# Seven block products for eight in one pair of output chunks of batches 2 to 7, with both packed casts of a slot on ScalarE

## The chip, the cores and the metric

The kernel runs on one core of a Trainium2 chip. The metric is the device time of one execution in microseconds. TensorE multiplies matrices into PSUM, VectorE (DVE) and ScalarE (ACT) do elementwise work and read PSUM, GpSimd (POOL) does elementwise work in SBUF and issues the input transfers, SyncE (SP) issues the output transfers and the transposing transfers.

## The reference

Attention through 32 packed vectors per head, then a layer with h * cos(h) as its activation. There are 8 batches, 8 heads, 576 tokens, a head width of 64; the layer is 512 -> 2048 -> 512 over 4608 tokens.

```python
p_packed = sm_attn(p, k, v)                  # 32 packed vectors per head
out = sm_attn(q, p_packed, p_packed)         # back to 576 tokens
x = transpose(out, (0, 2, 1, 3)).reshape(B * S, H * D)
h = x @ w_in                                 # 512 -> 2048
g = h * cos(h)
return g @ w_out                             # 2048 -> 512
```

## The kernel before

The packed vectors are multiplied by w_in first (PPW), so that h comes straight from the second attention's weights a2n and PPW. All matmuls take bf16 and sum in fp32. The kernel goes through the batches in steps. Step s computes attention and g of batch s, while TensorE is kept fed from a "filler": the output matmuls of batch s-1. A step has a front (scores, sums, normalisation, with pieces of filler) and a slot (16 h products, each followed by a quota of filler). PSUM has three double-bank tiles "psA" and two single banks "ot".

```python
A = ctx.enter_context(tc.tile_pool(name="psA", bufs=3, space=PSUM))
O = ctx.enter_context(tc.tile_pool(name="psO", bufs=2, space=PSUM))
...
def normalise(b):
    a2n[b] = a2n_pool.tile([128, 2, S], BF16, name="a2n", tag="a2n")
    for y in range(2):
        ACT.activation(out=lns[b][:, y], in_=lns[b][:, y], func=AF.Exp, scale=-1.0)
    for y in range(2):
        V.scalar_tensor_tensor(out=a2n[b][:, y], in0=a2u[b][:, y], scalar=r1[b][:, y:y + 1],
                               in1=lns[b][:, y], op0=ALU.mult, op1=ALU.mult)
...
def h_mm(b, fc):
    ps = psa()
    for y in range(2):
        for e in range(2):
            nc.tensor.matmul(ps[:, e, 0:HS], PPW[b][:, y, fc * 128:(fc + 1) * 128],
                             a2n[b][:, y, e * HS:(e + 1) * HS], start=(y == 0), stop=(y == 1))
    ...
    ACT.activation(out=csv, in_=ps[:, :, 0:HS], func=AF.Sin, bias=PI_HALF)
    def rest():
        V.tensor_tensor(out=gT[b][:, fc, :]..., in0=ps[:, :, 0:HS], in1=csv, op=ALU.mult)
        if fc % 8 == 7:          # the last 64 tokens go to a tile shared by two batches
            G.tensor_copy(out=joint[b // 2][...], in_=gT[b][:, fc - 7:fc + 1, 512:576])
    return rest
...
def out_gen(b):                  # the filler: chunks of 128 tokens, 512 columns at a time
    groups = [(0, 1), (2,), (3,)] if b == 0 else [(c,) for c in range(n_chunks(b))]
    for grp in groups:
        pss = {c: O.tile([128, DM], FP32, name="ot", tag="ot") for c in grp}
        ...
            nc.tensor.matmul(pss[c], w, w_out_bf[:, fc, :], start=(fc == 0), stop=(fc == NFC - 1))
            if fc == NFC - 1:
                copy(out_eng[...], osb, pss[c]); nc.sync.dma_start(out=rows, in_=osb[a:z, :])
            yield                # one unit of filler
```

Chunk 4 (the joint tile of two batches) is computed whole with the odd batch, so that a batch has 4 or 5 chunks of 16 units. A step from 3 on is:

```python
fill(1000); set_filler(s - 1)
permute_v(s + 1)                              # GpSimd
s2(s); ppw(s, 2, V); xbar("q", s + 1)
fill(10)
s1(s + 1); ppw(s, 3, V); a1_xbar(s + 1); recips(s + 1); ...
fill(4);  sums2(s, 0)
fill(5);  sums2(s, 1)
normalise(s)
ACT.preload_act_table_set(SIN_SET)
fill(13)
load(...)                                     # v, q of s + 2, k of s + 3
slot(s, [(5, lambda: pp(s + 1, engs=(ACT, ACT))), (10, lambda: pw2(s + 1))], 5, {10: 3})
```

In the slot, pp (the packed vectors of the next batch) comes after h 5 and pw2 (two packed products with their casts to bf16, one by VectorE and one by ScalarE) after h 10. The last line leaves five units for the end of the slot and gives h 10 a fourfold share.

Of the kernel before, what the change touches and what calls it, by code (L numbers as in the profile page):

```python
# [8 lines left out]
FP32 = mybir.dt.float32  # L9
# [6 lines left out]
def kernel(  # L16
# [10 lines left out]
    nc = tc.nc  # L27
    B, H, S, D = q.shape
# [5 lines left out]
    TP = S // C  # L34
    HS = S // 2
    PSUM = bass.MemoryType.PSUM
    EXP_SET = "natural_log_exp_and_others"
    SIN_SET = "trig_and_small"

    const = ctx.enter_context(tc.tile_pool(name="const", bufs=1))  # L40
    bf_pool = ctx.enter_context(tc.tile_pool(name="bf", bufs=1))
    vp_pool = ctx.enter_context(tc.tile_pool(name="vp", bufs=2))
    att_pool = ctx.enter_context(tc.tile_pool(name="att", bufs=1))
    a2n_pool = ctx.enter_context(tc.tile_pool(name="a2n", bufs=2))
    ppw_pool = ctx.enter_context(tc.tile_pool(name="ppw", bufs=2))
    g_pool = ctx.enter_context(tc.tile_pool(name="g", bufs=2))
    j_pool = ctx.enter_context(tc.tile_pool(name="joint", bufs=2))
    cos_pool = ctx.enter_context(tc.tile_pool(name="cos", bufs=3))
    o_pool = ctx.enter_context(tc.tile_pool(name="o", bufs=4))
# [8 lines left out]
    w_out_bf = const.tile([128, NFC, DM], BF16, name="w_out_bf")  # L58
    ident = const.tile([128, 128], BF16, name="ident")
# [3 lines left out]
    p_raw = const.tile([128, 2 * B, D], FP32, name="p_raw")  # L63
# [84 lines left out]
    def recips(b):  # L148
        r1[b] = small.tile([128, 2], FP32, name="r1")
        rs1[b] = small.tile([128, 2], FP32, name="rs1")  # L150
        V.reciprocal(r1[b], sums1[b])
        V.tensor_scalar(out=rs1[b], in0=r1[b], scalar1=scale, scalar2=None, op0=ALU.mult)
# [42 lines left out]
    def ppw(b, n, eng=None, own=False, later=False, cuts=((0, 512),)):  # L195
        if b not in PPW:
            PPW[b] = ppw_pool.tile([128, 2, DF], BF16, name="PPW", tag="PPW")
        two = isinstance(eng, tuple)
        if own:
            ps = [bank(), bank()]  # L200
        else:
            t = psa()
            ps = [t[:, 0, :], t[:, 1, :]]
        for x in range(4):
            for y in range(2):
                r = slice(64 * y, 64 * y + 64)
                nc.tensor.matmul(ps[y][32 * x:32 * x + 32, :], ppT[b % 2][r, 2 * x + y, :],  # L207
                                 w_in_bf[r, x, n * 512:(n + 1) * 512], start=True, stop=True)

        def evacuate(cuts=cuts):  # L210
            if own or two:
                for a, z in cuts:
                    for y in range(2):
                        copy(eng[y] if two else eng, PPW[b][:, y, n * 512 + a:n * 512 + z], ps[y][:, a:z])
            else:
                copy(eng or (V, ACT)[n % 2], PPW[b][:, :, n * 512:(n + 1) * 512], t)
        if later:
            return [lambda c=c: evacuate((c,)) for c in cuts]
        evacuate()

    def s2(b):
        a2u[b] = att_pool.tile([128, 2, S], BF16, name="a2u", tag="a2u")
        ps = scores(ppT[b % 2], xT["q", b])
        for y in range(2):
            ACT.activation(out=a2u[b][:, y].rearrange("p (e x) -> p e x", e=2),  # L225
                           in_=ps[y][:, :, 0:HS], func=AF.Exp, scale=rs1[b][:, y:y + 1])

    def sums2(b, y):
        if b not in lns:
            lns[b] = att_pool.tile([128, 2, S], FP32, name="lns", tag="lns")  # L230
        ps = psa()
        for e in range(2):
            nc.tensor.matmul(ps[:, e, 0:HS], ones_blk, a2u[b][:, y, e * HS:(e + 1) * HS],  # L233
                             start=True, stop=True)
        ACT.activation(out=lns[b][:, y].rearrange("p (e x) -> p e x", e=2),  # L235
                       in_=ps[:, :, 0:HS], func=AF.Ln)

    def normalise(b):
        a2n[b] = a2n_pool.tile([128, 2, S], BF16, name="a2n", tag="a2n")
        for y in range(2):  # L240
            ACT.activation(out=lns[b][:, y], in_=lns[b][:, y], func=AF.Exp, scale=-1.0)  # L241
        for y in range(2):
            V.scalar_tensor_tensor(out=a2n[b][:, y], in0=a2u[b][:, y], scalar=r1[b][:, y:y + 1],  # L243
                                   in1=lns[b][:, y], op0=ALU.mult, op1=ALU.mult)
# [3 lines left out]
    def h_mm(b, fc):  # L248
        if fc == 0:
            gT[b] = g_pool.tile([128, NFC, S], BF16, name="gT", tag="gT")  # L250
            if b % 2 == 0:
                joint[b // 2] = j_pool.tile([128, NFC, 128], BF16, name="joint", tag="joint")
        ps = psa()
        for y in range(2):
            for e in range(2):
                nc.tensor.matmul(ps[:, e, 0:HS], PPW[b][:, y, fc * 128:(fc + 1) * 128],  # L256
                                 a2n[b][:, y, e * HS:(e + 1) * HS], start=(y == 0), stop=(y == 1))
        cs = cos_pool.tile([128, S], BF16, name="cosT")
        csv = cs.rearrange("p (e x) -> p e x", e=2)
        ACT.activation(out=csv, in_=ps[:, :, 0:HS], func=AF.Sin, bias=PI_HALF)  # L260

        def rest():
            V.tensor_tensor(out=gT[b][:, fc, :].rearrange("p (e x) -> p e x", e=2),  # L263
                            in0=ps[:, :, 0:HS], in1=csv, op=ALU.mult)
            if fc % 8 == 7:
                j0 = (b % 2) * 64
                G.tensor_copy(out=joint[b // 2][:, fc - 7:fc + 1, j0:j0 + 64],  # L267
                              in_=gT[b][:, fc - 7:fc + 1, 512:576])
        return rest

    n_out, out_eng = [0], [V, ACT]

    def pieces_of(b, c):
        ob = out[b * S:(b + 1) * S, :].rearrange("(p c) d -> c p d", c=C)
        if c == 4:
            o0 = out[(b - 1) * S:b * S, :].rearrange("(p c) d -> c p d", c=C)
            return [(0, 64, o0[5, 32:96]), (64, 128, ob[5, 32:96])]
# [8 lines left out]
    def n_chunks(b):  # L286
        return 5 if b % 2 and b < B - 1 else 4

    def tail_chunk(b, c):
        osb = o_pool.tile([128, DM], FP32, name="osb")  # L290
        for i in range(2):
            cols = slice(i * 256, i * 256 + 256)
            ps = O.tile([128, 256], FP32, name="ot", tag="ot")
            for fc in range(NFC):
                nc.tensor.matmul(ps, joint[b // 2][:, fc, :], w_out_bf[:, fc, cols],  # L295
                                 start=(fc == 0), stop=(fc == NFC - 1))
            copy((ACT, V)[i], osb[:, cols], ps)
            for (a, z, rows), q in zip(pieces_of(b, c), (nc.sync, nc.scalar)):
                q.dma_start(out=rows[:, cols], in_=osb[a:z, cols])

    def out_gen(b):
        groups = [(0, 1), (2,), (3,)] if b == 0 else [(c,) for c in range(n_chunks(b))]
        for grp in groups:
            pss = {c: O.tile([128, DM], FP32, name="ot", tag="ot") for c in grp}
            for f0 in range(0, NFC, 4):
                for c in grp:
                    for fc in range(f0, f0 + 4):
                        w = joint[b // 2][:, fc, :] if c == 4 else gT[b][:, fc, c * 128:(c + 1) * 128]
                        nc.tensor.matmul(pss[c], w, w_out_bf[:, fc, :],  # L309
                                         start=(fc == 0), stop=(fc == NFC - 1))  # L310
                        if fc == NFC - 1:
                            osb = o_pool.tile([128, DM], FP32, name="osb")
                            copy(out_eng[n_out[0] % len(out_eng)], osb, pss[c])
                            n_out[0] += 1
                            for a, z, rows in pieces_of(b, c):
                                nc.sync.dma_start(out=rows, in_=osb[a:z, :])
                        yield
# [3 lines left out]
    def set_filler(b):  # L321
        fill(1000)
        filler[0] = out_gen(b)
        filler[1] = 16 * n_chunks(b)

    def fill(n):
        while n > 0 and filler[1] > 0:
            next(filler[0])
            filler[1] -= 1
            n -= 1  # L330

# [25 lines left out]
    wz = const.tile([128, 512], BF16, name="wz")  # L357
# [21 lines left out]
    recips(0)  # L379
    pp(0)  # L380
# [23 lines left out]
    for fc in range(NFC):  # L404
# [6 lines left out]
        if fc == 3:  # L411
            recips(1)
        if fc == 10:
# [6 lines left out]
    def slot(s, hooks, keep=0, heavy={}):  # L420
# [3 lines left out]
        for fc in range(NFC):  # L424
            h_mm(s, fc)()
            quota = (left * sum(weight[:fc + 1])) // sum(weight) - (left + keep - filler[1])
            first = quota
            while hooks and hooks[0][0] == fc:
                if first == quota and fc in heavy:
                    first = quota // 2  # L430
                    fill(first)
                hooks.pop(0)[1]()
            fill(quota - first if first != quota else quota)

    def pw2(b, n=0, eng=None):
        ppw(b, n, eng)
        ppw(b, n + 1, eng)

# [3 lines left out]
    def next_loads():  # L442
        G.tensor_copy(out=gate, in_=xT["k", 3][0:1, 0, 0:1])
        for n, b in (("q", 3), ("k", 4), ("v", 3)):
# [17 lines left out]
    slot(1, [(3, lambda: pw2(1, 2, (ACT, V))), (4, lambda: (xbar("q", 2), xbar("k", 3))), (5, tk("k", 2, 0)), (6, tk("k", 2, 1)),  # L462
             (7, tk("k", 2, 2)), (9, lambda: pack_p(2, 4)), (12, next_loads)], 4, {3: 3})
# [3 lines left out]
    fill(1000)  # L467
    set_filler(1)
# [8 lines left out]
    fill(7)  # L477
    s2(2)
# [17 lines left out]
    normalise(2)  # L496
    ACT.preload_act_table_set(SIN_SET)
    fill(8)
# [5 lines left out]
    fill(8)  # L504
    slot(2, [(7, lambda: pp(3, engs=(ACT, ACT))), (11, lambda: pw2(3))], 5, {11: 3})

    for s in range(3, B):
# [3 lines left out]
        fill(1000)  # L511
        set_filler(s - 1)
# [21 lines left out]
        normalise(s)  # L534
        ACT.preload_act_table_set(SIN_SET)
        fill(13)
# [3 lines left out]
        slot(s, [(5, lambda: pp(s + 1, engs=(ACT, ACT))), (10, lambda: pw2(s + 1))] if nxt else [], 5, {10: 3})  # L540
    out_eng[:] = V, ACT
    set_filler(B - 1)
    fill(1000)
    tail_chunk(B - 1, 4)
# [30 lines left out]
```

The softmax here doesn't subtract the row's maximum and nothing guards it: scores larger than these inputs give would overflow.

## Time and profile before

| quantity | value |
|---|---|
| time, median of 3 runs | 248.51 us (248.44 to 248.76) |
| span of the profiled execution | 246.8 us |
| output matmuls, 128x512, from gT | 482 recorded, from 35.9 us on |
| h matmuls, 128x288 | 512, from 21.8 to 223.7 us |
| gT product on VectorE | 128, 755 ns each |
| cosine on ScalarE | 128, 652 ns each |
| vp copy on GpSimd | 7, 2751 ns each |

A busy time counts an instruction from its start to its end. Matmuls overlap, so their mean duration is longer than what one costs; the distance of two starts shows the cost. In a timeline each line has start, duration, engine, source line, operation, tiles and count; what stands in square brackets is idle time of the engine before it and what ended it. L309 is the output matmul, L256 the h matmul, L295 the matmul of the very last chunk, L243 the a2n product, L233 the sums, L77 and L75 the copies by VectorE and ScalarE.

### The profile page before, as it was taken

The page shows a single profiled execution, that of the slowest core. Times are in us where ns is not written, and L with a number is a line of the kernel's source. Part 1 is how long each engine was busy: PE and PEld are TensorE (multiplying, and loading weights), DVE is VectorE, ACT ScalarE, POOL GpSimd, SP SyncE. Part 2 cuts the span into 40 slices and gives each one's busy share as a digit, 9 for nine tenths or more (in the row PEclk, how much of TensorE's full clock was granted, in tenths as well). Part 3 has the DMA queues.
Part 4 walks back from the last instruction along what each step waited for, and adds up shares of the span by engine and source line. Part 5 has one row for each costly group of instructions (what it writes and reads, how often), then busy time and mean ns, then how long its engine had stood idle before and what let it go on. Part 6 is the DMA issues. An engine that isn't in the chain of part 4 may idle for free.

```text
span 246.8 us, 5023 instructions
## 1 busy us (share of the span) xinstructions
PE 233.2 (94%) x1996; PEld 130.9 (53%) x2029; DVE 165.2 (67%) x248; ACT 169.0 (68%) x282; POOL 57.7 (23%) x70
## 2 busy tenths in 40 slices
PE   8788799999999999999999999999999999999993
PEld 3454374566545654565446554565456554665452
DVE  3549987677658776678767766678766684886110
ACT  2369799877576787888787776888778684873000
POOL 8342533240400355004503105030500100001000
PEclk9999999999999999999999999999999999999999
DMA  6999999999899999999999997999571113111133
GB/s 90 202 203 206 205 206 228 194 241 151 179 202 184 192 175 214 218 198 142 222 211 187 172 201 91 198 166 171 109 154 27 45 43 84 43 31 57 47 84 85
DMA packets 64231, 37.36 MB, mean 151 GB/s; under 512 B 36848, under 2 KB 59632, under 8 KB 64208
## 3 DMA queue, kind: packets, MB, share of 16 engines
q0 software_dynamic: 23152, 18.75, 50.0%
q1 hardware_dynamic: 40624, 18.09, 35.1%
q8 instruction: 16, 0.26, 0.4%
q10 hardware_dynamic: 432, 0.20, 0.4%
q14 instruction: 7, 0.06, 0.1%
HBM read 37.22 MB, written 9.44 MB: 189 GB/s over the span
## 4 chain that ended last, share of the span: by engine, by line
PE 78%; DMA 12%; issue 2%; DVE 2%; ACT 2%; POOL 2%; DVEq 0%; POOLq 0%
PE ot L309 46%; PE psA L256 21%; DMA vbf<-in_v_dram 10%; PE psA L207 3%; DMA a1T<-a 2%; PE psA L129 2%; PE psA L183 2%; DVE gT L263 2%; PE ot L295 1%; PE psA L233 1%; ACT cosT L260 1%; POOL vp L77 1%; ACT ppT L75 1%; POOL kbf L84 1%; PE ot L104 0%
## 5 line engine op out<-in xcount | busy, mean ns | idle before, releaser
L309 PE MATMUL ot<-w_out_bf,gT 128*128 128x512 bf16 x482 | 127.5, 379 | 2.0 <-issue 1.1
L263 DVE TENSOR_TENSOR gT<-psA,cosT 128x576 bf16<-128x576 f32 x128 | 93.8, 755 | 28.9 <-ACT cosT L260 28.2
L260 ACT ACTIVATE cosT<-psA 128x576 bf16<-128x576 f32 x128 | 82.4, 652 | 24.6 <-PE psA L256 22.1
L256 PE MATMUL psA<-a2n,PPW 128*128 128x288 bf16 x512 | 83.8, 286 | 1.6 <-DVE gT L263 0.4
L309 PEld LDWEIGHTS <-gT 128*128 128x128 bf16 x512 | 47.8, 98 | 43.4 <-issue 6.7
L256 PEld LDWEIGHTS <-PPW 128*128 128x128 bf16 x512 | 49.3, 98 | 34.6 <-issue 3.9
L77 DVE CAST PPW<-psA 128x1024 bf16<-128x1024 f32 (+1 forms) x23 | 26.9, 1175 | 11.6 <-PE psA L207 11.5
L267 POOL COPY joint<-gT 128x512 bf16<-128x512 bf16 x16 | 9.9, 616 | 82.5 <-DVE gT L263 82.5
L77 DVE COPY osb<-ot 128x512 f32<-128x512 f32 (+1 forms) x22 | 14.9, 678 | 17.5 <-PE ot L309 7.7
L77 POOL COPY vp<-vbf 96x3072 bf16<-96x3072 bf16 x7 | 19.3, 2751 | 6.3 <-DMA vbf<-in_v_dram 6.3
L75 ACT COPY osb<-ot 128x512 f32<-128x512 f32 (+1 forms) x15 | 8.5, 567 | 15.3 <-PE ot L309 10.6
L243 DVE SCALAR_TENSOR_TENSOR a2n<-a2u,r,lns 128x576 bf16<-128x576 bf16 x16 | 12.3, 812 | 7.3 <-ACT lns L241 7.3
L235 ACT ACTIVATE lns<-psA 128x576 f32<-128x576 f32 x16 | 10.1, 650 | 7.1 <-PE psA L233 6.5
L140 ACT ACTIVATE a<-psA 128x576 bf16<-128x576 f32 x16 | 10.3, 647 | 6.7 <-PE psA L129 6.7
L309 PE MATMUL ot<-w_out_bf,joint 128*128 128x512 bf16 x47 | 12.8, 379 | 0.1
L225 ACT ACTIVATE a2u<-psA,rs 128x576 bf16<-128x576 f32 x16 | 11.0, 737 | 1.4 <-PE psA L129 1.3
L75 ACT CAST ppT<-psA 64x128 bf16<-64x128 f32 x24 | 6.2, 260 | 7.0 <-DVE ppT L77 5.9
L207 PE MATMUL psA<-w_in_bf,ppT 64*32 64x512 bf16 x224 | 10.1, 380 | 0.0
L241 ACT ACTIVATE lns<-lns 128x576 f32<-128x576 f32 x16 | 10.0, 676 | 0.0
L347 PE MATMUL ot<-wz 128*128 128x512 bf16 x23 | 7.7, 468 | 1.4 <-DVE wz L358 1.2
L527 POOL COPY gate<-kT 1x1 bf16<-1x1 bf16 x3 | 0.5, 181 | 32.3 <-DMA kT<-kbf 32.3
L183 PEld LDWEIGHTS <-vp 96*128 96x128 bf16 x192 | 6.5, 98 | 2.3 <-issue 1.2
(73 smaller groups left out, 152.7 us busy)
## 6 DMA issues: line engine op xcount, KB each, us to landing
kbf<-in_k_dram POOLq DMA_DIRECT2D x8, 576.0 KB, 12.6
vbf<-in_v_dram POOLq DMA_DIRECT2D x8, 576.0 KB, 7.6
qbf<-in_q_dram POOLq DMA_DIRECT2D x8, 576.0 KB, 10.1
out_dram<-osb SPq DMA_DIRECT2D x24, 192.0 KB, 2.7
out_dram<-osb SPq DMA_DIRECT2D x22, 128.0 KB, 2.4
w_in_bf<-in_moe_w_in_dram POOLq DMA_DIRECT2D x4, 512.0 KB, 17.3
w_out_bf<-in_moe_w_out_dram POOLq DMA_DIRECT2D x4, 512.0 KB, 21.2
out_dram<-osb SPq DMA_DIRECT2D x26, 64.0 KB, 2.1
```

Source lines behind the costliest of these rows:

```text
L75: ACT.copy(out=out, in_=in_)
L77: eng.tensor_copy(out=out, in_=in_)
L140: ACT.activation(out=a1[b % 2][:, y, :, 0:TP].rearrange("p (e m) x -> p e m x", e=2), in_=ps[y][:, :, 0:HS].rearrange("p e (m x) -> p e m ...
L183: nc.tensor.matmul(ps[:, hp * 64:(hp + 1) * 64], vp[b][:, c, hp * 128:(hp + 1) * 128], a1T[b][0:TP, :, j, 32 * hp:32 * hp + 32], start=(j ...
L207: nc.tensor.matmul(ps[y][32 * x:32 * x + 32, :], ppT[b % 2][r, 2 * x + y, :], w_in_bf[r, x, n * 512:(n + 1) * 512], start=True, stop=True)
L225: ACT.activation(out=a2u[b][:, y].rearrange("p (e x) -> p e x", e=2), in_=ps[y][:, :, 0:HS], func=AF.Exp, scale=rs1[b][:, y:y + 1])
L235: ACT.activation(out=lns[b][:, y].rearrange("p (e x) -> p e x", e=2), in_=ps[:, :, 0:HS], func=AF.Ln)
L243: V.scalar_tensor_tensor(out=a2n[b][:, y], in0=a2u[b][:, y], scalar=r1[b][:, y:y + 1], in1=lns[b][:, y], op0=ALU.mult, op1=ALU.mult)
L256: nc.tensor.matmul(ps[:, e, 0:HS], PPW[b][:, y, fc * 128:(fc + 1) * 128], a2n[b][:, y, e * HS:(e + 1) * HS], start=(y == 0), stop=(y == 1))
L260: ACT.activation(out=csv, in_=ps[:, :, 0:HS], func=AF.Sin, bias=PI_HALF)
L263: V.tensor_tensor(out=gT[b][:, fc, :].rearrange("p (e x) -> p e x", e=2), in0=ps[:, :, 0:HS], in1=csv, op=ALU.mult)
L309: nc.tensor.matmul(pss[c], w, w_out_bf[:, fc, :], start=(fc == 0), stop=(fc == NFC - 1))
```

## The change

Two chunks of output are a product of a 256 x 2048 block with a 2048 x 512 block. Cut both in two by two blocks and the Winograd form of Strassen's method gives the four result blocks from seven block products instead of eight. It needs sums of blocks on both sides ahead, and sums of products behind. The sums of w_out (T) are made once, those of gT (S) for each batch; both are on GpSimd. The sums behind are on VectorE, which reads the products from PSUM. The aim is less work for TensorE. Chunks 0 and 1 of batches 2 to 7 go this way; the filler's order is chunk 2, half of a joint chunk, the pair, chunk 3. Units of filler become half units (a 256-column matmul).

```diff
-            ACT.activation(out=lns[b][:, y], in_=lns[b][:, y], func=AF.Exp, scale=-1.0)
...
+        if b < 3: ...                       # lns in SBUF as before
+        else:
+            lns[b, y] = ps[:, :, 0:HS]      # ln and exp stay in PSUM
...
+            t = lns[b, y]
+            ACT.activation(out=t, in_=t, func=AF.Exp, scale=-1.0)
+        def product(y): V.scalar_tensor_tensor(...)
+        if later:
+            return product
...
+    def S_sums(b, p, eng, k0, k1, which=(0, 1, 2, 3)):
+        A11, A12 = (A_blk(b, 2 * p, i, k0, k1) for i in range(2))
+        A21, A22 = (A_blk(b, 2 * p + 1, i, k0, k1) for i in range(2))
+            out, in0, in1, op = ((S1, A21, A22, ALU.add), (S2, S1, A11, ALU.subtract),
+                                 (S3, A11, A21, ALU.subtract), (S4, A12, S2, ALU.subtract))[i]
+            eng.tensor_tensor(out=out, in0=in0, in1=in1, op=op)
...
+    def pair_gen(b, p):
+        m = {1: (A11, B_blk(0, 0)), 2: (A12, B_blk(1, 0)), 3: (S4, B_blk(1, 1)),
+             4: (A_blk(b, 2 * p + 1, 1, 0, 8), T[3]), 5: (S1, T[0]), 6: (S2, T[1]), 7: (S3, T[2])}
+        then = {1: lambda ps: copy(out_eng[0], m1, ps), 2: lambda ps: plus(o1[:, 0:3:2, :], ps, m1),
+                7: lambda ps: plus(u3, ps, o1[:, 2]), 4: then_double, 3: then_last}
+        for names in ((1,), (2, 6), (7,), (4, 5), (3,)):
+            ps = O.tile([128, 2, 256], FP32, name="ot", tag="ot")
+            for i, n in enumerate(names):
+                lhs, rhs = m[n]
+                for kp in range(8):
+                    nc.tensor.matmul(ps[:, i], lhs[:, kp, :], rhs[:, kp, :], start=kp == 0, stop=kp == 7)
...
+        yield from direct_gen(b, ((2, ), (3, )) if last else ((2,),))
+        for g in joints:                    # 16 matmuls of 256 columns, then a copy by out_eng
+            yield from g
+        yield from pair_gen(b, 0)
+        if not last:
+            yield from direct_gen(b, ((3,),))
...
+    def close(s):
+        fill(1000)
+        if s >= FIRST:
+            for g in ((6, 8),) if s == B - 1 else ((0, 4), (4, 8)):
+                S_sums(s, 0, G, *g)
+        set_filler(s)
+    def pw2_late(b):
+        ppw(b, 0, ACT)
+        late.extend(ppw(b, 1, ACT, later=True))
...
-        fill(1000)
-        set_filler(s - 1)
+        close(s - 1)
...
-        normalise(s)
+        product = normalise(s, later=True)
         ACT.preload_act_table_set(SIN_SET)
-        fill(13)
+        fill(4)
+        product(0)
+        product(1)
+        fill(9)
...
-        slot(s, [(5, lambda: pp(s + 1, engs=(ACT, ACT))), (10, lambda: pw2(s + 1))] if nxt else [], 5, {10: 3})
+        slot(s, [(2, lambda: scaled(s + 1)), (5, lambda: pp(s + 1, engs=(ACT, ACT))), (10, lambda: pw2_late(s + 1)), (11, lambda: late.pop()())] if nxt else [], 8, {10: 3})
```

Besides: the joint chunk is computed in two halves of 256 columns, one with each of two neighbouring batches. The scaling rs1 moves from VectorE (in recips) to ScalarE (scaled, after h 2). In a slot the gT product of an h is put into VectorE's queue after the quota of filler instead of ahead of it. The vp tile has one buffer instead of two, and PPW is held in quarters (four buffers) instead of whole (two). The T sums run in steps 1 and 2 on GpSimd. The last batch's S sums run partly inside slot 7, and its output begins with chunks 2 and 3.

## Prediction

> **What bounds the kernel now.** I began with the page's first two parts. TensorE is busy for 94% of the span and its clock is full in every slice, so the time is the sum of TensorE's work plus what it waits for.
>
> ```profile
> PE 233.2 (94%) x1996; PEld 130.9 (53%) x2029; DVE 165.2 (67%) x248; ACT 169.0 (68%) x282; POOL 57.7 (23%) x70
> PE   8788799999999999999999999999999999999993
> PEclk9999999999999999999999999999999999999999
> PE 78%; DMA 12%; issue 2%; DVE 2%; ACT 2%; POOL 2%; DVEq 0%; POOLq 0%
> ```
>
> The last line is the chain that ended last: 78% is TensorE. Its DMA share lies in the first 30 us (the loads of the first batches), where the change does nothing.
>
> A mean duration of a matmul is no cost, because matmuls overlap. I took costs from starts in TensorE's own order of time:
>
> ```profile
> 153.15 1.24 PE L309 MATMUL ot<-w_out_bf,gT 128*128 128x512 bf16 x5
> 154.23 0.41 PE L233 MATMUL psA<-a2u,ones_blk 128*128 128x288 bf16 x2
> 154.48 2.97 PE L309 MATMUL ot<-w_out_bf,gT 128*128 128x512 bf16 x12
> 157.28 0.65 PE L256 MATMUL psA<-a2n,PPW 128*128 128x288 bf16 x4
> 157.77 0.38 PE L309 MATMUL ot<-w_out_bf,gT 128*128 128x512 bf16 x1
> ...
> 239.16 3.66 PE L295 MATMUL ot<-w_out_bf,joint 128*128 128x256 bf16 x32
> ```
>
> The program issues 13 matmuls of 512 columns from 154.48 to 157.28 (12 are recorded): 2.80/13 = 0.2155 us each. Four of 288 take 0.49 us, 0.1227 each. In the last chunk 32 of 256 columns start between 239.16 and 242.5, and 3.3/31 = 0.107 us each. So a narrow matmul with new weights every time still costs just half of a wide one.
>
> Now the steady state, batch step s = 5. From its first score matmul at 148.60 to its first h matmul at 157.28 are 8.68 us; the work there is 32 x 0.2155 = 6.90 plus about 1.65 of scores, packed products and sums (read from the gaps between starts). From there to 173.82 are 16.54 us; the work is 64 x 0.1227 = 7.85, 32 x 0.2155 = 6.90, and about 1.4 of packed products, together 16.15. TensorE waits for only about 0.5 us in 25. Removing TensorE work therefore pays fully, and any new wait on TensorE costs fully.
>
> What stands beside the front of such a step, on VectorE:
>
> ```profile
> 153.78 0.69 DVE L77 COPY osb<-ot 128x512 f32<-128x512 f32 x1
> 155.93 1.55 DVE L243 SCALAR_TENSOR_TENSOR a2n<-a2u,r,lns 128x576 bf16<-128x576 bf16 x2 [1.46 <-ACT lns L241]
> 157.48 0.69 DVE L77 COPY osb<-ot 128x512 f32<-128x512 f32 x1
> ```
>
> VectorE idles 1.46 us for ScalarE's exponentials, makes both halves of a2n by 157.48, and only then copies the next finished output chunk. In the kernel before nobody needs that chunk's bank yet.
>
> **What the skill says.** "TensorE: Matmul & The Clock Gate", Back-to-back issue gap, gives N/2.4 + 2.5 ns for an isolated matmul: 109 ns for 256 columns and 216 for 512. The trace agrees (107, 215.5). "PSUM — Partial Sum Buffer", Engine vs sequencer instructions, says that ScalarE, VectorE and GpSimd queues are strict FIFO; the three lines just shown agree, the copy of a finished chunk standing behind a waiting product. "GPSIMD Engine Reference", Performance versus the Vector engine, has 4497 ns for a two-input add of 2048 fp32 elements, so 512 elements are 1.1 us and I take 1.2 as an estimate; no two-input operation of GpSimd is in this trace. "SBUF — State Buffer", Who interferes with whom, says that VectorE instructions with two SBUF inputs contend with GpSimd's reads. The change reads ln values out of PSUM from batch 3 on, so that the products keep off that port; no run here shows the contention.
>
> **Part 1: seven products for eight.** Two chunks now are 32 x 0.2155 = 6.90 us. The pair is 7 x 8 = 56 matmuls of 256 columns, 56 x 0.107 = 5.99. Saved: 0.90 us per pair, six pairs, **-5.4 us**. Splitting a joint chunk into two halves of 16 narrow matmuls is neutral (32 x 0.107 = 3.42 against 16 x 0.2155 = 3.45).
>
> **Part 2: the sums on GpSimd.** Eight adds of 512 elements per batch at 1.2 us are 9.6 us, begun when gT is complete and its joint copy done (149.1 in step 5's time). They end about 158.7, and permute_v (2.75 us) then ends about 161.5; its reader, the product pp, came at 161.80. Just in time, no cost. The second half of S2 is the sixth add, ready at 156.3, before product 6 needs it in the slot. The four T sums (2048 elements, 4.5 us each) lie in GpSimd's idle time of steps 1 and 2, but T2 (about 72.8 to 77.3) overlaps the two-SBUF-input product of batch 2 at 76.3 to 77.8: I allow **+0.5 us**, once.
>
> **Part 3: a new wait for an output bank.** There are two "ot" banks. Before the slot the filler now runs chunk 2 (16 wide), the joint half (16 narrow), product 1 (8), product 2 (8). Product 2 takes the bank of the joint half, so it waits for that half's copy. Counting: the fills of 10, 4 and 5 units are 38 half units, 32 for chunk 2 and 6 of the joint half. The fill of 4 brings the half to 14 of 16. Then both products of a2n are put into VectorE's queue, and only after them, in the fill of 9, come the last two matmuls and the copy. With the times above: sums end at 154.48, the joint half at 154.48 + 10 x 0.107 = 155.55, product 1 at 156.40; the copy can't start before about 157.45 and takes 0.42 (the 128x256 copy at the end of the kernel took 0.424). Product 2 starts near 157.85 instead of 156.40: **1.45 us per step, in the five steps 3 to 7, +7.2 us**. The slot behind it starts later by as much, and being TensorE-bound it gives nothing back.
>
> **Part 4: both packed casts on ScalarE.** A 128x1024 cast takes 1.01 us on ScalarE, 1.22 on VectorE; now they run side by side. After the change ScalarE has cast, cosine, cast in a row. From the start of h 10: packed products end at 1.7, cast one at 2.6, cosine 11 runs 3.15 to 3.8, cast two to 4.8. h 13 takes the bank of cast two, and TensorE reaches it at 4.1: about 0.7 us lost, where the trace shows some 0.2 now. **+0.5 us in four steps, +2.0.**
>
> **Part 5: the adds on VectorE.** A pair needs about 2.6 us of adds besides one 0.42 copy (0.69 for 512 columns, 0.42 for 256, like the copies) where two copies were 1.38; a cast of 1.22 and a 0.2 us scaling leave it. VectorE has about 14.8 us in a slot of 16 to 17, ScalarE 14.9. The adds are queued ahead of a product that still waits for its cosine, so I count nothing in the slot. At the end, with nothing beside the pair, products 4 and 5 and the last chunk wait for adds: **+0.5**.
>
> Sum: -5.4 + 0.5 + 7.2 + 2.0 + 0.5 = **+4.8, 253.3 us**.
>
> **Rivals.** (a) The saving comes through and the bank wait does not, because ScalarE's exponentials in PSUM are quicker or the copy finds an earlier place: -5.4 + 2.0 + 1.0 or less, 243.5 to 246. For it: the saving is plain TensorE arithmetic, and reading ln in PSUM and moving the scaling off VectorE look like deliberate care. Against it: the order of the queue is fixed by the program, and 1.46 us of idle VectorE before the product is in the trace. (b) The slot becomes bound by ScalarE and VectorE, both near 0.88 of it, with only three psA banks for a turn of about 2.3 us (0.49 + 0.2 + 0.7 + 0.1 + 0.8) at 0.85 us per h. Small waits in every slot, +1 us each, would make it 255 or more. Against it: the slot of step 5, with 16 h in 16.54 us, waits for under 0.4 us in all with the same three banks. (c) GpSimd's adds take 1.6 us instead of 1.2; then permute_v is late and pp waits about 1.5 us in each of four steps. The bank wait of part 3 moves pp later by as much and so hides it.
>
> **Range and chances.** I give the bank wait about three chances in four at full size and rival (a) the rest; between 253.3 and 246 that puts my time at **252.0 us**, range **246.0 to 255.5**. Faster by over 2% means under 243.6, which needs the whole saving without a wait: 0.05. Slower by over 2% means over 253.5, my sum with a little of rival (b): 0.33. Within 2%: 0.62.
>
> **What would show it.** Part 1: 336 matmuls of 128x256 in the pairs, starts 0.107 us apart where they follow each other. Part 3: in steps 3 to 7 the first matmul of product 2 idle about 1.4 us, released by a VectorE copy of osb that stands straight behind the a2n products. Part 4: TensorE idle before h 13, released by ScalarE's cast. Part 2: no wait of pp for vp and none of product 6 for S. I am wrong if that copy runs ahead of the products, if a GpSimd add is far from 1.2 us, or if the narrow matmuls do not keep their 0.107 us inside the slot.

## The result, and the profile after

The changed kernel takes 258.82 us (258.72 to 258.87, 3 runs) against 248.51: ratio 1.0412, 95% interval 1.0388 to 1.0435. It is 10.3 us slower, where 252.0 had been predicted and 246.0 to 255.5 given as the range. The span of the profiled execution grew by 9.8 us, from 246.8 to 256.6.

The page's first parts and its chain, for the changed kernel:

```profile
PE 232.6 (91%) x2199; PEld 149.8 (58%) x2221; DVE 167.7 (65%) x268; ACT 170.3 (66%) x289; POOL 128.1 (50%) x126
PE   8778799999999999898979999898989998999993
PEclk9999999999999999999999999999999999999999
PE 64%; DVE 12%; DMA 10%; ACT 7%; issue 5%; POOL 0%; DVEq 0%; ACTq 0%; POOLq 0%
```

The clock is full, so no clock explains it. From the middle on, TensorE's row has an 8 or a 7 in every step where it had only nines. In the chain TensorE fell from 78% to 64%, VectorE rose from 2% to 12% and ScalarE from 2% to 7%: work that stood beside TensorE now stands between two of its matmuls. GpSimd rose from 23% to 50% busy and has no share of the chain.

TensorE's order of time at the front of step 5 (start, duration, then the group; L332 is the joint half, L406 the pair, L272 the h matmul), and the start of the last chunk:

```profile
157.63 0.41 PE L243 MATMUL psA<-a2u,ones_blk 128*128 128x288 bf16 x2
157.87 1.25 PE L332 MATMUL ot<-w_out_bf,joint 128*128 128x256 bf16 x10
158.97 1.04 PE L406 MATMUL ot<-w_out_bf,gT 128*128 128x256 bf16 x8
161.26 1.03 PE L406 MATMUL ot<-w_out_bf,gT 128*128 128x256 bf16 x8 [1.26 <-DVE osb L81]
162.13 0.65 PE L272 MATMUL psA<-a2n,PPW 128*128 128x288 bf16 x4
...
248.86 3.67 PE L332 MATMUL ot<-w_out_bf,joint 128*128 128x256 bf16 x32 [0.24 <-DVE osb L379]
```

Ten narrow matmuls take 1.10 us from start to start and eight of product 2 take 0.87, so one costs 0.109 us; the prediction had 0.107. Product 1 begins at 158.97 and would have made room for product 2 at 159.84; it starts at 161.26. The page's idle time of 1.26 counts from the modelled end of the matmul before, so the loss on TensorE is 1.42. In steps 3 to 7 it is 1.42, 1.49, 1.42, 1.42 and 1.37.

VectorE in the same stretch:

```profile
159.33 1.54 DVE L255 SCALAR_TENSOR_TENSOR a2n<-a2u,r,psA 128x576 bf16<-128x576 bf16 x2 [1.47 <-ACT psA L251]
160.79 0.42 DVE L81 COPY osb<-ot 128x256 f32<-128x256 f32 x1
```

The joint half was complete at 159.0. Its copy stands behind two products that wait for ScalarE, and runs at 160.79. That is part 3 of the prediction as written.

What the prediction did not have is in the slot. Three waits recur in steps 3 to 6 at the same places (L189 is pp, L212 a packed product):

```profile
167.21 0.86 PE L189 MATMUL psA<-a1T,vp 96*128 96x64 bf16 x24 [0.23 <-DVE gT L279]
...
173.14 0.41 PE L212 MATMUL psA<-w_in_bf,ppT 64*32 64x512 bf16 x8
173.82 0.41 PE L212 MATMUL psA<-w_in_bf,ppT 64*32 64x512 bf16 x8 [0.28 <-DVE gT L279]
174.16 0.55 PEld L354 LDWEIGHTS <-gT 128*128 128x128 bf16 x4 [0.23 <-issue]
174.39 0.81 PE L354 MATMUL ot<-w_out_bf,gT 128*128 128x512 bf16 x3 [0.16 <-issue]
...
177.22 0.65 PE L272 MATMUL psA<-a2n,PPW 128*128 128x288 bf16 x4 [0.39 <-DVE gT L279]
```

The first is pp: h 5 ended its issue at 166.81, so 0.40 us are lost. The second packed product follows 0.68 behind the first where each needs 0.29: 0.39 lost. Then h 13 loses 0.55. Together 1.34 us in each of four steps. In the slot of step 5 before, pp lost 0.07 and h 9 lost 0.24.

The 0.28 us between the second packed product and the next group look like a fourth wait and are not one. TensorE loaded weights for four matmuls there (the PEld line) and three are recorded, so one record of 0.216 us is missing, and about 0.06 is left. The same four loads and three records stand in steps 3, 4 and 6. Some expectations below count the 0.28 as lost, and so come to 1.07 us a step for pp and the packed products; it is 0.85.

From first score matmul to first score matmul, steps 3 to 6 took 26.80 us on average before (94.95 to 202.16, over 4) and take 28.83 now (94.20 to 209.53). That step 3 starts 0.75 us earlier is no gain: half a joint chunk (about 1.7 us) that step 2 worked on before is now in step 7. Without it the changed kernel is about 1.0 behind by then.

### The profile page after: what moved, and what is told of

It reads as the page before. It is cut to its first block, busy times and chain, and to the rows that moved or that the text cites. A ratio compares the mean times of both kernels' runs of the same rounds, so it can differ in the third digit from the quotient of the medians.

```text
span 256.6 us, 5549 instructions
## 1 busy us (share of the span) xinstructions
PE 232.6 (91%) x2199; PEld 149.8 (58%) x2221; DVE 167.7 (65%) x268; ACT 170.3 (66%) x289; POOL 128.1 (50%) x126
## 4 chain that ended last, share of the span: by engine, by line
PE 64%; DVE 12%; DMA 10%; ACT 7%; issue 5%; POOL 0%; DVEq 0%; ACTq 0%; POOLq 0%
PE ot L354 24%; PE psA L272 16%; PE ot L406 10%; DMA qbf<-in_q_dram 7%; DVE gT L279 5%; ACT cosT L276 5%; PE ot L332 5%; DMA vbf<-in_v_dram 3%; DVE osb L379 3%; PE psA L212 3%; PE psA L189 2%; PE psA L133 2%; DVE a2n L255 2%; PE psA L243 1%; DVE osb L81 1%
## 5 line engine op out<-in xcount | busy, mean ns | idle before, releaser
L272 PE MATMUL psA<-a2n,PPW 128*128 128x288 bf16 x512 | 83.5, 286 | 3.3 <-DVE gT L279 2.2
L354 PE MATMUL ot<-w_out_bf,gT 128*128 128x512 bf16 x300 | 79.9, 379 | 2.1 <-issue 1.7
L272 PEld LDWEIGHTS <-PPW 128*128 128x128 bf16 x512 | 49.2, 98 | 26.0 <-issue 6.9
L313 POOL TENSOR_TENSOR S<-gT 128x512 bf16<-128x512 bf16 (+1 forms) x26 | 28.0, 1078 | 1.3 <-PE ot L406 1.3
L406 PE MATMUL ot<-T,S 128*128 128x256 bf16 x144 | 22.6, 273 | 0.0
L406 PEld LDWEIGHTS <-S 128*128 128x128 bf16 x192 | 18.8, 98 | 3.3
L406 PEld LDWEIGHTS <-gT 128*128 128x128 bf16 x144 | 13.8, 98 | 9.3 <-issue 7.2
L406 PE MATMUL ot<-w_out_bf,gT 128*128 128x256 bf16 x96 | 12.3, 272 | 6.3 <-DVE osb L81 6.3
L332 PE MATMUL ot<-w_out_bf,joint 128*128 128x256 bf16 x128 | 16.3, 273 | 0.2 <-DVE osb L379 0.2
L313 POOL TENSOR_TENSOR S<-S,gT 128x512 bf16<-128x512 bf16 (+1 forms) x13 | 14.0, 1078 | 1.0
L332 PEld LDWEIGHTS <-joint 128*128 128x128 bf16 x128 | 12.5, 98 | 3.2 <-DVE osb L379 0.5
L313 POOL TENSOR_TENSOR S<-gT,S 128x512 bf16<-128x512 bf16 (+1 forms) x13 | 14.0, 1078 | 0.0
L255 DVE SCALAR_TENSOR_TENSOR a2n<-a2u,r,psA 128x576 bf16<-128x576 bf16 x10 | 7.7, 812 | 7.4 <-ACT psA L251 7.4
```

Source lines behind the costliest of these rows:

```text
L255: V.scalar_tensor_tensor(out=v[0], in0=v[1], scalar=r1[b][:, y:y + 1], in1=lns[b, y], op0=ALU.mult, op1=ALU.mult)
L272: nc.tensor.matmul(ps[:, e, 0:HS], PPW[b, fc // 4][:, y, fc % 4 * 128:fc % 4 * 128 + 128], a2n[b][:, y, e * HS:(e + 1) * HS], start=(y == ...
L313: eng.tensor_tensor(out=out, in0=in0, in1=in1, op=op)
L354: nc.tensor.matmul(pss[c], gT[b][:, fc, c * 128:(c + 1) * 128], w_out_bf[:, fc, :], start=(fc == 0), stop=(fc == NFC - 1))
L406: nc.tensor.matmul(ps[:, i], lhs[:, kp, :], rhs[:, kp, :], start=kp == 0, stop=kp == 7)
```

## Experiments

Theory: TensorE lost time to the order of work in VectorE's and ScalarE's queues: a copy behind products, adds ahead of gT products, a cast behind a cosine. Rivals: GpSimd's new adds slow VectorE or come late; the slot is bound by ScalarE and VectorE anyway, so that a wait taken away comes back elsewhere; or the other parts of the change are to blame and not the pair. All edits are to the changed kernel; ratios are to the kernel before, run on the same chip.

### The copy ahead of the products

```diff
-        fill(4)
+        fill(5)
         product(0)
         product(1)
-        fill(9)
+        fill(8)
```

> The joint half's last two matmuls and its copy are put ahead of the two a2n products (fills of 5 and 8 units instead of 4 and 9). Queue theory (TensorE waits because of the order of work in VectorE's and ScalarE's queues): the wait of 1.42 us before product 2 goes in five steps, but the copy now delays the a2n products by about 0.3 us, so 5 x 1.1 = 5.5 us less: 253.3 us. Rival, the slot is bound by ScalarE and VectorE: the slot merely starts earlier and waits longer, 257.5 to 258.8 us.

Measured: 252.44 us, ratio 1.0156 (1.0135 to 1.0178), 6.4 us less than the changed kernel.

```profile
155.61 1.25 PE L332 MATMUL ot<-w_out_bf,joint 128*128 128x256 bf16 x10
156.70 1.91 PE L406 MATMUL ot<-w_out_bf,gT 128*128 128x256 bf16 x16
158.44 0.78 PE L272 MATMUL psA<-a2n,PPW 128*128 128x288 bf16 x4
```

Products 1 and 2 now are one unbroken run of 16, 1.74 us from start to start; 0.13 of the wait stays in each step, at the second half of the first h. One unit of filler moved across two lines gives back 6.4 us. The rival that the slot takes up the gain is refuted for this wait.

### The second cast at once

```diff
     def pw2_late(b):
         ppw(b, 0, ACT)
-        late.extend(ppw(b, 1, ACT, later=True))
+        ppw(b, 1, ACT)
...
-(11, lambda: late.pop()())
+(11, lambda: None)
```

> ScalarE casts the second packed product directly after the first instead of after h 11. Queue theory: ScalarE was idle there for 1.1 us and h 13 waits 0.55 us for the bank of that cast, so 4 x 0.5 = 2 us less: 256.8 us. Rival, h 13 waits for VectorE's gT product as the profile names it: no gain, 258.5 to 259.5 us.

Measured: 256.50 us, ratio 1.0326 (1.0302 to 1.035), 2.3 us less. ScalarE in the changed kernel shows the room that the cast now uses:

```profile
173.62 1.01 ACT L79 CAST PPW<-psA 128x1024 bf16<-128x1024 f32 x1 [0.49 <-PE psA L212]
175.73 0.65 ACT L276 ACTIVATE cosT<-psA 128x576 bf16<-128x576 f32 x1 [1.10 <-PE psA L272]
176.28 1.01 ACT L79 CAST PPW<-psA 128x1024 bf16<-128x1024 f32 x1
```

ScalarE idles 1.10 us before cosine 11, and only then casts the bank that h 13 needs. The page had put h 13's wait down to a gT product, which ends at the same moment as the cast; the run decides for the cast.

### The gT product ahead of the filler's quota

```diff
             if not (hooks and hooks[0][0] == fc):
-                fill_halves(quota)
                 rest()
+                fill_halves(quota)
```

> The gT product of an h goes into VectorE's queue ahead of the quota of filler, so ahead of the pair's adds, as in the kernel before. Queue theory: pp and the second packed product no longer wait for a delayed gT (0.40, and 0.39 with 0.28 behind it), 4 x 0.8 = 3 us less: 255.7 us. Rival, the adds then come too late and TensorE waits for a bank of the output instead: 258 to 260 us.

Measured: 259.22 us, ratio 1.0434 (1.0408 to 1.0461): no gain, as the rival said. In its trace:

```profile
167.31 0.86 PE L189 MATMUL psA<-a1T,vp 96*128 96x64 bf16 x24 [0.23 <-DVE gT L279]
...
173.24 0.63 PE L212 MATMUL psA<-w_in_bf,ppT 64*32 64x512 bf16 x16
174.19 1.02 PE L354 MATMUL ot<-w_out_bf,gT 128*128 128x512 bf16 x3 [0.32 <-DVE osb L379]
```

The two packed products now run together, but the next output chunk waits 0.36 us for an add (L379) to free its bank, and 1.05 us at the same place in step 7, where the changed kernel lost 0.12. pp's wait is as before, since at h 2, where "scaled" is hooked, both orders put that add behind gT 2 and ahead of gT 3. So the order alone is not the cause; the adds take their time from one chain or the other.

### Everything but the pair

```diff
-    FIRST = 2
+    FIRST = B
...
-                if s == B - 1 and fc in (10, 13):
+                if FIRST < B and s == B - 1 and fc in (10, 13):
```

> All of the change but the pair: chunks 0 and 1 are plain in every batch, no S sums; the T sums still run, casts, scaling, queue order and half joint chunks stay. Queue theory: 5.4 us more matmul work, but no wait for the joint half's copy (7.1), none for the pair's adds in the slot (4 x 1.1 = 4.4) nor at the end (0.6): 258.8 + 5.4 - 12.1 = 252.1 us, still some 2 us over the kernel before for the late cast and 1 us in the first two steps. Rival, the other parts (casts on ScalarE, normalisation in PSUM, one vp buffer) cost most of the loss: 255 us or more.

Measured: 251.75 us, ratio 1.0136 (1.0111 to 1.0161). In this run the filler takes chunks 0 to 3 in order and the joint half last. With 4.8 us more matmul work (0.80 in each of six pairs, with narrow matmuls at 0.109) it is 7.1 us faster. The other parts together cost 3.3 us over the kernel before: its steps 3 to 6 take 27.41 us each (94.55 to 204.20, over 4) against 26.80, four times 0.61, and about 1 us is lost ahead of step 3. Most of the 0.61 is the late cast: h 13 waits 0.56 in each of these steps here too.

### The pair without GpSimd's sums

```diff
-            for g in ((6, 8),) if s == B - 1 else ((0, 4), (4, 8)):
-                S_sums(s, 0, G, *g)
+            pass
...
-        S1, S2, S3, S4 = (S[b, p][:, i] for i in range(4))
+        S1, S2, S3, S4 = (A_blk(b, 2 * p + i // 2, i % 2, 0, 8) for i in range(4))
```

The calls inside slot 7 are left out too.

> The pair without its S sums: blocks of gT stand in for S1 to S4, so the output is not the reference's; 56 adds of GpSimd are left out, all else stays. Queue theory: GpSimd is off every path that TensorE waits for; permute_v ends over 2 us before pp, so nothing changes: 258.5 to 259 us. Rival, GpSimd's adds slow VectorE[...], or make vp late: 255 us or less.

Measured: 259.00 us, ratio 1.0424 (1.0398 to 1.045), the same as the changed kernel's. (52 adds are left out, not the 56 of the expectation: the page has 126 instructions of GpSimd for the changed kernel and 74 here.) GpSimd is off the path and the GpSimd rival falls. In the changed kernel its last add of step 5 ends at 161.97, and the vp copy is

```profile
161.92 2.74 POOL L81 COPY vp<-vbf 96x3072 bf16<-96x3072 bf16 x1
```

so vp is ready 2.5 us before pp reads it.

### Copy and cast together

The edits of the first two experiments in one kernel.

> The copy ahead of the products and the cast at once, together. If the two waits are separate terms of one sum on TensorE, their gains add: 258.8 - 6.4 - 2.3 = 250.1 us. Rival, both only uncover the same limit of the slot: 251.5 us or more.

Measured: ratio 1.0091 (1.0064 to 1.0118), which is 250.6 us on 248.4; one of its six executions, at a lower granted clock (0.987) and 255.54 us, is left out. Taken one by one the two save 8.7 us; together 8.2. They are separate terms of a sum within the interval, whose upper end (251.3) is still under the rival's 251.5.

### Small adds

```diff
-            V.tensor_tensor(out=out, in0=in0, in1=one, op=ALU.add)
+            V.tensor_tensor(out=out[..., 0:32], in0=in0[..., 0:32], in1=one[..., 0:32], op=ALU.add)
```

The stores of the pair are cut to the same 32 columns; seven eighths of these adds and stores are left out.

> The changed kernel with the pair's adds on 32 of every 256 columns and only those stored, so seven eighths of the pair's adds and stores are left out; all matmuls, copies and their order stay. Theory that the adds delay gT products and bank releases by their own length: pp's wait of 0.40, the wait of the second packed product with 0.39 and 0.28 behind it, both in four steps, and 0.65 at the end go: 258.8 - 4.3 - 0.6 = 253.9 us. Rival, those waits come from the turn of three psA banks alone, whatever VectorE does between: 258 us or more.

Measured: 254.61 us, ratio 1.0243 (1.0218 to 1.0269), 4.2 us less than the changed kernel. The same places in its trace:

```profile
165.69 0.86 PE L189 MATMUL psA<-a1T,vp 96*128 96x64 bf16 x24
...
171.55 0.63 PE L212 MATMUL psA<-w_in_bf,ppT 64*32 64x512 bf16 x16
...
245.18 3.66 PE L332 MATMUL ot<-w_out_bf,joint 128*128 128x256 bf16 x32
```

No wait over 0.06 us is left at pp, between the packed products or at the last chunk. The bank wait at product 2 (1.42 in step 5) and the wait of h 13 (0.56) stayed. The stores are shorter in this run too, but they explain no wait in the slots: in the changed kernel one add in 30 waits for a store (9.4 us, the first add of the last pair, after 9.4 us in which VectorE had nothing to do), and none in a slot. So the adds' own length on VectorE costs 4.2 us. The waits that went are 4 x 0.72 and 0.65 at the end, 3.5 us of the 4.2; the other 0.7 is about the width of the interval. The expected 4.9 had the missing record in it, 4 x 0.22.

### pp and the packed products spread

The first experiment's edit, and

```diff
-(5, pp), (10, pw2_late), (11, late.pop()), ... 8, {10: 3}
+(5, pp), (10, ppw(s + 1, 0, ACT)), (11, ppw(s + 1, 1, ACT)), ... 8, {5: 1, 10: 1, 11: 1}
```

(shortened). An h named in the last braces gets a double quota, half of it ahead of its hook.

> The copy ahead of the products; and in the slot pp comes in the middle of a double quota after h 5, and the two packed products come one after h 10 and one after h 11, each in the middle of a double quota with its cast on ScalarE directly behind. If the waits left are TensorE arriving at a bank while VectorE still works off adds and gT, matmuls put ahead of pp and between the packed products cover them: of 1.07 us per step about 0.9 go, and the late cast's 0.55, so 252.4 - 4 x 1.45 = 246.6 us, under the kernel before. Rival, VectorE and ScalarE are full in the slot and the waits come back at other h: 249.5 us or more.

Measured: 248.50 us, ratio 1.0012 (0.9998 to 1.0026): level with the kernel before, but not the 246.6 expected. Up to 0.9 of that gain was the missing record and not there to be had. The covers worked at pp (0.07 us lost) and at h 13 (none), but (TensorE first, then VectorE):

```profile
166.69 0.49 PE L406 MATMUL ot<-w_out_bf,S 128*128 128x256 bf16 x3
167.32 0.41 PE L212 MATMUL psA<-w_in_bf,ppT 64*32 64x512 bf16 x8
...
165.59 0.68 DVE L379 TENSOR_TENSOR osb<-ot,u 128x512 f32<-128x512 f32 x1
166.52 1.41 DVE L279 TENSOR_TENSOR gT<-psA,cosT 128x576 bf16<-128x576 f32 x2
```

Three narrow matmuls end their issue at 167.02, and the packed product comes 0.30 later. It takes the bank of h 8. Cosine 8 ended at 165.80, but gT 8 starts at 166.52, behind the adds of products 4 and 5, and ends at about 167.2.

### The packed products one h later

As before, with the hooks at 11 and 12.

> As e8_spread, but the packed products come after h 11 and h 12 instead of h 10 and h 11, when VectorE has worked off the adds of products 4 and 5. In e8_spread the first packed product still waits 0.3 us in each of four steps. If that is VectorE's backlog of adds: 248.5 - 4 x 0.3 = 247.3 us, under the kernel before. Rival, the wait follows the packed product wherever it is: 248.5 us.

Measured: 249.12 us, ratio 1.0031 (1.0016 to 1.0046), no gain.

```profile
166.53 0.49 PE L406 MATMUL ot<-w_out_bf,S 128*128 128x256 bf16 x3
167.17 0.65 PE L272 MATMUL psA<-a2n,PPW 128*128 128x288 bf16 x4
```

The 0.3 us did not vanish and did not follow the packed product either. They stay with the bank of h 8, whose gT product is behind the same adds (it starts at 166.36 here); h 11 takes that bank now. Neither of the two readings above holds as worded: it is VectorE's backlog, but it meets whatever comes next.

### The spread without the pair

The kernel of the last experiment with the edit of "Everything but the pair".

> e9_spread_later with plain chunks 0 and 1 in every batch, so without the pair and its sums. If the pair's saving on TensorE (5.4 us, less 0.65 at the end) comes through once its waits are covered, this is 4 us or more above e9_spread_later: 251.5 us. If most of the saving still goes into waits, it is within 2 us of it: 249.5 us or less.

Measured: 250.57 us, ratio 1.0081 (1.0064 to 1.0098), 1.45 us more than with the pair by the medians and 1.2 by the ratios, so within 2 us of it: most of the saving still goes into waits. Of 4.8 us of matmul work that the pair removes, 1.2 to 1.5 arrive when its waits are mostly covered. Steps 3 to 6 are 27.00 us without the pair (94.28 to 202.26) and 26.67 with it (94.06 to 200.72): 0.33 us a step of the 0.80 removed. The rest is in the trace with the pair and not in the other: in step 5 it waits 0.31 at h 11, 0.13 inside the first h and 0.07 at pp.

## Why the prediction was wrong

**Seven products for eight, -5.4 us: right in kind, a little too large.** 16 narrow matmuls behind each other took 1.74 us (0.109 each), and as much in the slot, mixed with h. The prediction's 0.107 came from 3.3 us for 31 starts, read off a time in tenths; 56 x 0.109 = 6.10 against 6.90 saves 0.80 a pair, 4.8 in six.

**GpSimd's sums: right in the steps, wrong in the allowance.** An add of 512 took 1.15 us (estimate 1.2), and leaving all of them out changed nothing. The 0.5 us for a contention of T2 with the product of batch 2 did not come: T2 ended at 76.16, the product began at 76.91 and took 1.54, as before. By luck this error and that of 0.6 us on the seven products nearly cancel.

**The wait for the joint half's bank, +7.2 us: right.** 7.1 us in five steps, for the reason given; moving the copy gave back 6.4.

**The late cast, +2.0 us: right.** h 13 lost 0.55 in each of four steps, and doing the cast at once gave back 2.3.

**The adds on VectorE, 0.5 us: this step failed.** Part 5 said "The adds are queued ahead of a product that still waits for its cosine, so I count nothing in the slot." VectorE in the slot of step 5, with the cosines (ACT) that the two gT products wait for:

```profile
165.38 0.65 ACT L276 ACTIVATE cosT<-psA 128x576 bf16<-128x576 f32 x1 [0.18 <-PE psA L272]
165.81 0.68 DVE L379 TENSOR_TENSOR osb<-ot,m 128x512 f32<-128x512 f32 x1
166.41 0.75 DVE L279 TENSOR_TENSOR gT<-psA,cosT 128x576 bf16<-128x576 f32 x1
...
171.66 0.65 ACT L276 ACTIVATE cosT<-psA 128x576 bf16<-128x576 f32 x1 [0.28 <-PE psA L272]
172.09 0.68 DVE L379 TENSOR_TENSOR osb<-ot,u 128x512 f32<-128x512 f32 x1
172.69 0.41 DVE L379 TENSOR_TENSOR osb<-ot,osb 128x256 f32<-128x256 f32 x1
173.02 0.75 DVE L279 TENSOR_TENSOR gT<-psA,cosT 128x576 bf16<-128x576 f32 x1
```

Cosine 3 ended at 166.03, but gT 3 starts at 166.41, 0.4 later, behind an add; and pp wants the bank of gT 3. Cosine 9 ended at 172.31, but gT 9 starts at 173.02, 0.7 later, behind two adds; and the second packed product wants its bank. The adds came when the cosine was nearly or already done.

A share does not say whether a chain has slack: VectorE was busy for 13.59 of the 16.54 us of this slot before, and for 13.45 of 18.60 now, so its share fell while its adds cost time (the prediction counted 14.8 of 16 to 17). What decides is how long a psA bank is out, from the start of its h to the end of its gT product, against when TensorE comes back for it. For h 3 and h 9 the first is 2.47 and 2.80 us, and 2.09 for both without the delays of 0.38 and 0.71 behind adds. TensorE comes back 2.12 us after the start of h 3 (for pp, which stands ahead of h 5's quota) and 2.46 after that of h 9. So the first has no slack to speak of and the second under 0.4, and delays of 0.38 and 0.71 reach TensorE. The prediction had this turn in rival (b), at about 2.3 us, and set it aside because the slot before waited for under 0.4 us; but no adds stood in the chain there. Measured: 4.2 us in place of 0.5, of which 0.65 at the end, where the 0.5 had been placed, and the rest in the slots, where nothing had been counted.

The sum of the terms as the trace and runs size them: -4.8 + 7.1 + 2.3 + 4.2 + about 1.0 ahead of step 3 = 9.8, of 10.3 us by the medians and 9.8 in the span. The 1.0 is a step that the prediction did not have, and its cause stays open. 0.2 of it has come by the first score matmul of step 1 (38.24 before, 38.43 after) and 0.6 by that of step 2 (68.87 and 69.48). In the run without the pair step 2 also begins at 69.48, so the pair is not to blame for that part. (Of the DMA share of the chain before, 5.4 us lie at 79 us, in step 2, and not in the first 30 us as the prediction has it.) Finally, the point was set below the sum of 253.3, because one chance in four went to the bank wait not happening. The order of the queue, which the prediction had read rightly, left no such chance.

## What to carry to other kernels

Before handing an engine "only" small work inside a tightly turning pipeline, compare how long a buffer is out with when it is wanted again, and not the engine's busy share: here a bank that was out for 2.09 us was wanted after 2.12 and 2.46 us, so delays of 0.38 and 0.71 us behind adds cost TensorE 0.40 and 0.39, though VectorE was idle for over a quarter of the slot. An output copy that frees a scarce bank belongs in an in-order queue ahead of work that waits for another engine: two lines of order were worth 6.4 us here. And saved matmul work counts only after the waits it brings are subtracted: of 4.8 us, 1.2 to 1.5 arrived in the one improved placement that was run with and without the pair. Last, before a gap in a trace is called a wait, count the records: one missing matmul looked like 0.22 us of waiting in four steps, and carried an error of 0.9 us into three expectations.

## What the hardware showed unexpectedly

GpSimd's two-input bf16 adds took 0.67 us for 256 elements a partition, 1.15 for 512 and 4.06 for 2048, with no trace of a delay to VectorE: leaving out 52 adds moved the time by 0.2 us, within the runs' spread. The a2n product took 1.54 us for two, the same with its last input in PSUM (batch 3 on) as in SBUF (batch 2).
